# A long convolution as a two-stage 2048-point transform with relayout through DRAM, hardware gelu, resident weights and a list-scheduled order

## The chip, the cores and the metric

The kernel runs on one core of a Trainium2 chip. The metric is device time in microseconds (us); the profile's span is shorter by about 2 us. Engines: PE is TensorE (matmul), PEld its weight loads, DVE VectorE, ACT ScalarE, POOL GpSimd, SP the engine that issues most transfers. PSUM is the on-chip memory that the matmuls write (psall in the listings); SBUF holds the other tiles.

## The reference, cut to what matters

```python
x = A_q                                             # [1, 2048, 512] bf16
xn = _layernorm(x)
# A: causal 4-tap shift of k, times v, long convolution, gate by xn
k_shift = sum over t of k_pad[:, t:t+S, :] * shift_k[:, ks-1-t]
kv = k_shift * v
y = irfft(rfft(kv, 2S) * rfft(ssm_k, 2S))[:S] + kv * ssm_D      # per channel
s = xn * y
# B: gated feed-forward, Dm = 512, Df = 1792
h = gelu_tanh(xn @ w_gate) * (xn @ w_up)
g = silu(h @ w_down)
out = x + s * g
```

The feed-forward needs 448 + 224 matmuls of 128x128 weights by 512 columns. How many the convolution needs depends on the algorithm.

## The kernel before

The convolution is cut in four blocks of 512 rows. Each block is transformed by a dense 1024-point DFT matrix (built in the kernel), the blocks' spectra are multiplied pairwise on DVE, and each output block is one inverse transform:

```python
def fwd_passB_group(dlt, mr, bank):                 # filter spectra: 224 matmuls
    for i_, (kt, ht) in enumerate(kts):             # 4 or 8 per group
        trk.op("PE", lambda e, ...: e.matmul(PS[bank][:, :], lhsT=stat, rhs=HT_sb[:, ht, :], ...))
    trk.op("ACT", lambda e: e.activation(SPEC[:, HS(dlt), mr, :], PS[bank][:, :], ACTF.Identity, scale=wc), ...)
# ... fwd_passA_group: the same for kv, 128 matmuls

def build_products(c):                              # spectra, on DVE, 128x2048 bf16 each
    for k, (hs, ks) in enumerate(terms):            # c + 1 terms
        # ... four products into TMP, two to four sums into Yp

def inverse_mm_part(c, half):                       # 128 matmuls over all blocks
    # ... 8 matmuls per 128 output rows, rhs=Yp
```

GELU is built from ACT and DVE passes over 128x512 tiles, each `unit` being one of 56 (quarter of rows, block of Df):

```python
def g_A(u):   # PSUM (gate and up, 1024 columns) -> GUS                  ACT
def g_B1(u):  # SQ = (sqrt(a) g)^2                                       ACT
def g_T(u):   # SQ = SQ + 1                                              DVE
def g_B3(u):  # SQ = SQ * g                                              DVE
def g_C(u):   # SG = sigmoid(2c SQ)                                      ACT
def g_D(u):   # Wb = up * SG                                             DVE
def g_E(u):   # HTq = Wb * g                                             DVE
```

The program is emitted in a hand-made order: transforms first, then four quarters of the feed-forward with DVE's spectral products and the inverse transforms strewn between. Weights are loaded again for each quarter. A tracker puts in every semaphore wait from the tiles that an instruction reads and writes.

## Time and profile before

| | before |
|---|---|
| time, median (range) | 333.7 us (333.24 to 334.14) |
| span | 331.3 us |
| PE, DVE, ACT busy | 272.6, 266.2, 207.7 us |
| matmuls of 512 columns | 1160 |
| bytes moved | 34.8 MB |

From the page of the kernel before: busy time of each engine, three of the rows of 40 slices (a digit is the busy share of a slice of 8.3 us in tenths; PEclk is the granted TensorE clock in tenths), and the chain of waits that ended last.

```profile
PE 272.6 (82%) x1328; PEld 124.3 (38%) x1352; DVE 266.2 (80%) x473; ACT 207.7 (63%) x305; POOL 17.5 (5%) x33
...
PE   0235999999999969975878997968997998999970
...
DVE  6997899990069955999999899999999963766733
...
PEclk9999999999999979999999999999999999999995
...
PE 47%; DVE 35%; ACT 12%; issue 2%; DMA 2%; POOL 1%; POOLq 0%; ACTq 0%
```

PE is nearly full from the fifth slice on, with dents where DVE is full.

The groups of instructions by shape, kernel before: line, engine, operation, output<-inputs, shapes, count, then busy us and mean ns of one, then idle time before and what ended it.

```profile
L959 PE MATMUL psall<-XNTq,WBUF 128*128 128x512 bf16 x373 | 86.9, 383 | 11.1 <-ACT GUS L727 3.8 <-ACT XNTq L557 3.6 <-DMA WBUF<-in_B_w_gate_dram 2.7
L727 ACT ACTIVATE GUS<-psall 128x1024 bf16<-128x1024 f32 x56 | 56.8, 1014 | 22.7 <-PE psall L959 22.5
...
L436 DVE TENSOR_TENSOR TMP<-SPEC 128x2048 bf16<-128x2048 bf16 x40 | 47.5, 1215 | 19.3 <-ACT SPEC L604 19.3
...
L436 DVE TENSOR_TENSOR HTq<-Wb,GUS 128x512 bf16<-128x512 bf16 x56 | 23.8, 425 | 1.9
...
L436 DVE TENSOR_TENSOR G<-psall,SG 128x512 bf16<-128x512 f32 x16 | 9.9, 678 | 11.5 <-ACT SG L796 11.5
L436 DVE TENSOR_TENSOR XN_sb<-psall,XN_sb 128x1024 bf16<-128x1024 f32 x8 | 9.8, 1219 | 7.1 <-PE psall L812 7.1
```

A matmul's mean of 383 ns is the time from its start to its end in the profile, in which others run beside it. What it costs is the pitch, the time from one start to the next, which the windows show: busy time (and count) of PE, PEld, DVE, ACT, POOL, then clock, DMA share, GB/s.

```profile
40.00:60.00 20.00, 19.89 (x92) 9.09 (x93) 19.96 (x14) 8.24 (x12) 0.00 (x0) 1.00 0.00 0
...
160.00:200.00 40.00, 35.93 (x173) 16.00 (x176) 38.36 (x78) 25.50 (x38) 2.91 (x4) 1.00 0.41 129
```

92 matmuls in 19.9 us are 216 ns each. From 160 to 200 us both PE and DVE are almost full. So PE's 1160 matmuls alone are 250 us of the 331.

### The profile page before, as it was taken

The numbers are of one execution on the slowest core, as the hardware profiler recorded it, in microseconds if no ns is written. First come the engines' busy times: TensorE is split into PE (matmuls) and PEld (weight loads), VectorE is DVE, ScalarE is ACT, GpSimd is POOL, SyncE is SP. The second block draws the span as 40 slices with busy tenths as digits, with TensorE's granted clock in tenths as the row PEclk, the third lists the DMA queues.
The fourth block names the chain that finished last, engine by engine and source line by source line (L and its number), as shares of the span: only waits on it lengthen the run. The fifth ranks groups of instructions, "written<-read, shape, count | busy, mean of one in ns | idle before, by whom it ended". The sixth has DMA issues, their size and how long they took to land.

```text
span 331.3 us, 3631 instructions
## 1 busy us (share of the span) xinstructions
PE 272.6 (82%) x1328; PEld 124.3 (38%) x1352; DVE 266.2 (80%) x473; ACT 207.7 (63%) x305; POOL 17.5 (5%) x33
## 2 busy tenths in 40 slices
PE   0235999999999969975878997968997998999970
PEld 0005544444544424422333442424442344443420
DVE  6997899990069955999999899999999963766733
ACT  1498934443986745885629677637668928679820
POOL 2002300000000000000000200000020000120001
PEclk9999999999999979999999999999999999999995
DMA  7999200000000071534212745203643513653301
GB/s 243 264 252 256 65 1 0 2 0 0 2 0 0 2 253 31 161 127 128 96 34 94 232 161 177 74 23 127 190 120 136 160 63 127 190 141 116 95 0 63
DMA packets 52899, 34.83 MB, mean 105 GB/s; under 512 B 26257, under 2 KB 51858, under 8 KB 52882
## 3 DMA queue, kind: packets, MB, share of 16 engines
q1 hardware_dynamic: 51602, 30.42, 32.0%
q0 software_dynamic: 1280, 4.20, 3.9%
q8 instruction: 10, 0.16, 0.2%
q14 instruction: 7, 0.06, 0.0%
HBM read 26.22 MB, written 2.10 MB: 85 GB/s over the span
## 4 chain that ended last, share of the span: by engine, by line
PE 47%; DVE 35%; ACT 12%; issue 2%; DMA 2%; POOL 1%; POOLq 0%; ACTq 0%
PE psall L592 15%; PE psall L959 10%; DVE TMP L436 9%; PE psall L602 8%; PE psall L1034 8%; DVE Yp L436 7%; PE psall L812 4%; DVE HTq L436 4%; DVE Wb L436 3%; DVE SQ L436 3%; ACT GUS L727 3%; DVE G L436 2%; DVE SQ L737 2%; PE psall L531 2%; DVE XN_sb L436 2%
## 5 line engine op out<-in xcount | busy, mean ns | idle before, releaser
L959 PE MATMUL psall<-XNTq,WBUF 128*128 128x512 bf16 x373 | 86.9, 383 | 11.1 <-ACT GUS L727 3.8
L727 ACT ACTIVATE GUS<-psall 128x1024 bf16<-128x1024 f32 x56 | 56.8, 1014 | 22.7 <-PE psall L959 22.5
L436 DVE TENSOR_TENSOR TMP<-SPEC 128x2048 bf16<-128x2048 bf16 x40 | 47.5, 1215 | 19.3 <-ACT SPEC L604 19.3
L959 PEld LDWEIGHTS psall<-XNTq,WBUF 128*128 128x128 bf16 x384 | 36.6, 98 | 58.9 <-ACT GUS L727 9.4
L745 ACT ACTIVATE SG<-SQ 128x512 bf16<-128x512 bf16 x56 | 34.7, 621 | 26.9 <-DVE Wb L436 26.9
L592 PE MATMUL psall<-HT_sb,TT_sb 128*128 128x512 bf16 x219 | 48.1, 379 | 0.3
L1034 PE MATMUL psall<-WBUF,HTq 128*128 128x512 bf16 x188 | 43.4, 379 | 5.6 <-DVE HTq L436 5.2
L595 ACT ACTIVATE SPEC<-psall,COLS 128x512 bf16<-128x512 f32 x32 | 21.6, 700 | 25.3 <-PE psall L592 25.3
L733 ACT ACTIVATE SQ<-GUS 128x512 bf16<-128x512 bf16 x56 | 35.3, 630 | 1.8
L592 PEld LDWEIGHTS psall<-HT_sb,TT_sb 128*128 128x128 bf16 x224 | 21.9, 98 | 26.2
L1034 PEld LDWEIGHTS psall<-WBUF,HTq 128*128 128x128 bf16 x192 | 18.0, 98 | 30.4 <-DVE HTq L436 6.4
L812 PE MATMUL psall<-Yp,T_sb 128*128 128x512 bf16 x127 | 28.7, 379 | 0.1
L436 DVE TENSOR_TENSOR Yp<-Yp,TMP 128x2048 bf16<-128x2048 bf16 x24 | 28.5, 1215 | 0.0
L602 PE MATMUL psall<-KV_sb,TT_sb 128*128 128x512 bf16 x125 | 27.5, 379 | 0.4 <-ACT KV_sb L580 0.3
L567 DVE SCALAR_TENSOR_TENSOR acc<-kT_sb,SK,acc 128x2047 bf16<-128x2047 bf16 (+2 forms) x12 | 27.2, 2341 | 0.0
L737 DVE TENSOR_SCALAR SQ<-SQ 128x512 bf16<-128x512 bf16 x56 | 16.1, 288 | 12.2 <-ACT SQ L733 12.2
L436 DVE TENSOR_TENSOR HTq<-Wb,GUS 128x512 bf16<-128x512 bf16 x56 | 23.8, 425 | 1.9
L436 DVE TENSOR_TENSOR Wb<-GUS,SG 128x512 bf16<-128x512 bf16 x56 | 23.3, 415 | 0.2 <-ACT SG L745 0.2
L436 DVE TENSOR_TENSOR SQ<-SQ,GUS 128x512 bf16<-128x512 bf16 x56 | 23.2, 415 | 0.0
L604 ACT ACTIVATE SPEC<-psall 128x512 bf16<-128x512 f32 x32 | 18.7, 637 | 6.7 <-PE psall L602 6.7
L959 PE MATMUL psall<-XNTq,WDR 128*128 128x512 bf16 x64 | 15.2, 380 | 6.6 <-ACT GUS L727 6.6
L836 POOL DMA_DIRECT2D out_dram<-XR x8 | 5.9, 732 | 259.4 <-DVE XR L436 257.0
(65 smaller groups left out, 233.4 us busy)
## 6 DMA issues: line engine op xcount, KB each, us to landing
WBUF<-in_B_w_gate_dram SPq DMA_DIRECT2D x12, 512.0 KB, 3.8
WBUF<-in_B_w_up_dram SPq DMA_DIRECT2D x12, 512.0 KB, 4.8
WBUF<-in_B_w_down_dram SPq DMA_DIRECT2D x12, 512.0 KB, 3.8
X_sb<-in_A_q_dram SPq DMA_DIRECT2D x2, 1024.0 KB, 7.0
XR<-in_A_q_dram POOLq DMA_DIRECT2D x8, 256.0 KB, 3.3
out_dram<-XR POOLq DMA_DIRECT2D x8, 256.0 KB, 3.7
WDR<-in_B_w_gate_dram SPq DMA_DIRECT2D x4, 256.0 KB, 5.4
WDR<-in_B_w_up_dram SPq DMA_DIRECT2D x4, 256.0 KB, 2.8
```

Source lines behind the costliest of these rows:

```text
L436: trk.op(eng, lambda e: e.tensor_tensor(out_ap, a_ap, b_ap, op), r=r, w=w)
L567: trk.op("DVE", lambda e, kd=kd, sh=sh: e.scalar_tensor_tensor(out=acc[:, kd, sh:S_LEN], in0=kT_sb[:, kd, 0:S_LEN - sh], scalar=SK32[:, kd ...
L592: trk.op("PE", lambda e, kt=kt, ht=ht, stat=stat, i_=i_: e.matmul(PS[bank][:, :], lhsT=stat, rhs=HT_sb[:, ht, :], start=(i_ == 0), stop=(i ...
L595: trk.op("ACT", lambda e: e.activation(SPEC[:, HS(dlt), mr, :], PS[bank][:, :], ACTF.Identity, scale=wc), r=psr_all(bank) + [rCOLS], w=[rS ...
L602: trk.op("PE", lambda e, kt=kt, stat=stat: e.matmul(PS[bank][:, :], lhsT=stat, rhs=KV_sb[:, 4 * c + kt, :], start=(kt == 0), stop=(kt == 3 ...
L727: trk.op("ACT", lambda e: e.activation(GUS[:, sl, :], PS2(gb), ACTF.Copy), r=psr_2(gb), w=[rGUS[sl]])
L733: trk.op("ACT", lambda e: e.activation(SQ[:, sq, :], GSv(sl), ACTF.Square, scale=SQRT_A), r=[rGUS[sl]], w=[rSQ[sq]])
L737: trk.op("DVE", lambda e: e.tensor_scalar(SQ[:, sq, :], SQ[:, sq, :], 1.0, None, ALU.add), r=[rSQ[sq]], w=[rSQ[sq]])
L745: trk.op("ACT", lambda e: e.activation(SG[:, s2, :], SQ[:, sq, :], ACTF.Sigmoid, scale=GELU_2C), r=[rSQ[sq]], w=[rSG[s2]])
L812: trk.op("PE", lambda e, bank=bank, stat=stat, kr=kr: e.matmul(PS[bank][:, :], lhsT=stat, rhs=Yp[:, slot, kr, :], start=(kr == 0), stop=(k ...
L959: trk.op("PE", lambda e, bank=bank, stat=stat, kd=kd: e.matmul(PS[bank][:, :], lhsT=stat, rhs=XNTq[:, kd, :], start=(kd == 0), stop=(kd == ...
L1034: trk.op("PE", lambda e, bank=bank, mf=mf, jt=jt, buf=buf, mi=mi: e.matmul(PS[bank][:, :], lhsT=HTq[:, mf, 128 * jt:128 * (jt + 1)], rhs=b ...
```

## The change

Intent: fewer matmuls by a two-stage factorisation of the transform (16 x 128 points); relayout between the stages by writing scratch tensors to DRAM and reading them back in the other order; the product of the spectra taken straight from PSUM; gelu as one hardware function; weights loaded once; and an order found by a list scheduler in the program itself (tasks with estimated durations and priorities; it decides only the order of emission, the tracker still sets the waits). The core of the diff, cuts marked:

```diff
-        def g_A(u): ...   def g_B1(u): ...   def g_T(u): ...   def g_B3(u): ...
-        def g_C(u): ...   def g_D(u): ...    def g_E(u): ...
+        def unit(q, m):
+            # ... two halves of four matmuls each (gate, up) into one two-bank PSUM slot
+            op([("ACT", act(512))], lambda e, h: h.activation(GE[:, g.slot, :], ps(psl(p), 0), ACTF.Gelu_apprx_tanh), ...)
+            op([("DVE", dve(512, 1))], lambda e, h: h.tensor_tensor(HT[:, q % 2, m, :], ps(psl(p), 1), GE[:, g.slot, :], ALU.mult), ...)
-            # build_products, inverse_mm_part, fwd_passA_group, fwd_passB_group
+        def stage1(x, t, data, R_data, b_data, Z, prio):        # 16 times for the filter H, 16 for kv (K)
+            # ... 2 matmuls with F1[:, t, c, :] into a two-bank slot of pC
+            op([("ACT", act(1024)), ("DVE", dve(1024, 1))], ... copy(e, h, AST[:, a.slot, :, :]...))   # 3 staging buffers
+            S.add([("SP", 60.0)], st, r=[a], w=[bZ[x][t]], prio=prio, nbytes=262144)                    # store to ZH or ZK
+        for b in range(8):                                       # middle: load BH, BK from ZH, ZK
+            for pr in range(2):                                  # 16 steps
+                # K transform (2 matmuls, slot of pC) -> KB by ACT
+                # H transforms (2 + 2 matmuls, two slots) -> P1, P2 = PSUM * KB by DVE
+                # inverse (4 matmuls, a slot) -> BO by ACT or DVE -> store to ZI
+        # ... last stage: load BI from ZI, 32 matmuls, XN = PSUM * XN, output
+        pF = Pool_("psF", 2)                                     # PSUM slots of two banks each
+        pC = Pool_("psC", 2)
+        order = S.run()
+        for t in order:
+            t.emit(t.eng)
```

## The prediction

> **Now.** Span 331.3 us (page), 333.7 timed. PE busy 272.6 us, DVE 266.2, ACT 207.7 (busy table); the chain of waits is PE 47%, DVE 35%, ACT 12%. By windows: until 32 us DVE is full and PE nearly idle; from 40 to 100 us PE runs forward transforms at 216 ns a matmul (92 in 19.9 us); from 120 to 315 us PE is 84-98% busy, DVE full at 160-240.
>
> **The change, by program order.**
> PE: 512-column matmuls fall from 1160 to 928: gate/up 448 and down 224 stay, the convolution's 480 become 64 + 160 (middle) + 32 (last). At 216 ns that is 200 us, with 128 transposes about 210.
> DVE: spectral products (TMP, Yp: 86 us) and four GELU passes (SQ twice, Wb, HTq: 86 us) go. Added, at trace durations: 32 products PSUM x SBUF 128x1024 at 1.22 us (39 us); 56 HT multiplies at 0.68 us (38 us); 8 more PSUM passes (10 us). The shift is 32 passes of 1.215 us (39 us). Sum about 195.
> ACT: GELU becomes one 0.62 us pass instead of three (2.27 us); about 58 PSUM copies at 1.01 us. Sum about 120.
> DMA: weights load once, but three 4 MB scratch tensors are written and read: 40 MB, was 34.8. Each hop costs a landing of 2.6-3.8 us for 256-512 KB (DMA issue list); the Trainium skill, "DMA: Bandwidth & Descriptors" (anatomy of one DMA), gives about 2 us as fixed, and the trace agrees.
>
> **What lies on the critical path.** The order puts the engines partly in series:
> 1. Opening, DVE-bound. PE cannot start the first down projection before DVE has done tables, layernorm, 32 shift passes and 14 HT multiplies: tables and mask 15, layernorm 20, shift 39, evacuations 10, HT 9 = 93 us, plus about 11 of early waits for iotas and loads: 104 us (98-115). PE does only 144 of 928 matmuls here. The 14 MB of loads (50-55 us at the trace's 240-280 GB/s) and the stores queued behind should hide.
> 2. Then 696 matmuls x 216 ns = 150 us. The middle has four PSUM uses per step in two slots: an estimate of 4.2 us per step without interference, against 4.3-6 of PE work, so 12 us of stalls.
> 3. Tail: last scratch round trip mostly covered, then 88 matmuls (19 us) beside 21 us of DVE, last passes and landing: 29 us.
> Sum 295, plus 2.4 (timed minus span): **297 us, 281 to 318**, ratio 0.89.
>
> Chances: faster by over 2% 0.94, within 2% 0.03, slower 0.03.
>
> **What would show it.** DVE nearly full from 12 to 100 us, PE below half until 100, over 85% from about 105 to 265; the chain first DVE, then PE; HT 0.68 us, P products 1.22, GE 0.62; PE sum about 210, DVE 195; two ACT table loads, so gelu and tanh share one. Two-byte products from SBUF run at twice the rate of PSUM ones (Trainium skill, "VectorE: DVE Perf Modes", the perf-mode tier table; trace: 128x2048 SBUF 1215 ns, 128x1024 PSUM 1219); the shift's broadcast operand should keep that.
>
> **What would make it wrong.** Slower: broadcast or integer passes lose the fast rate (+17 to 25 us); stores queued behind the loads hold the three staging buffers and, through in-order ACT and PE, the first gate/up; two PSUM slots make the middle latency-bound at 6 us a step (+20). Faster: PE finds more to do in the opening, or no stalls in the middle: 280.

## The result, and the profile after

Ratios below are the mean time of one kernel's fast runs over that of the kernel before's fast runs of the same rounds, so not quite the ratio of the medians quoted. (The 333.7 us above was the median of three runs; here a fourth is added.)

| | before | after |
|---|---|---|
| time, median (range) | 333.85 us (333.24 to 334.14) | 279.62 us (278.94 to 280.19) |
| ratio | | 0.838 (0.836 to 0.841) |
| span | 331.3 us | 277.8 us |
| PE, DVE, ACT busy | 272.6, 266.2, 207.7 us | 218.3, 187.6, 118.1 us |
| matmuls of 512 columns | 1160 | 928 |
| bytes moved | 34.8 MB | 42.3 MB |

The direction was right; the time lies 1.4 us under the predicted range and 17 us under its centre. The page after (a slice is 6.9 us):

```profile
PE 218.3 (79%) x1056; PEld 100.9 (36%) x1056; DVE 187.6 (68%) x256; ACT 118.1 (43%) x141; POOL 17.4 (6%) x56
...
PE   0473003006999999999999999999999999999980
...
DVE  4999999897799953422332286767626477636996
...
PEclk9998555555999999999999999999999999999995
...
PE 74%; DVE 18%; ACT 2%; DMA 2%; POOL 1%; issue 1%; DVEq 0%
```

The reader sees two stretches with a sharp border in the tenth slice: before it DVE is full and PE idle, after it PE is at 9 without a dent. The prediction had PE "below half until 100".

Groups by shape, after:

```profile
L952 DVE TENSOR_TENSOR P<-psall,KB 128x1024 bf16<-128x1024 f32 x32 | 38.9, 1221 | 23.4 <-PE psall L519 22.9
L882 DVE TENSOR_TENSOR HT<-psall,GE 128x512 bf16<-128x512 f32 x56 | 38.3, 687 | 34.0 <-PE psall L519 33.8
L878 ACT ACTIVATE GE<-psall 128x512 bf16<-128x512 f32 x56 | 33.4, 597 | 41.7 <-PE psall L519 41.7
...
L847 DVE TENSOR_TENSOR KTM<-KK,SKB 128x2048 bf16<-128x2048 bf16 x12 | 14.6, 1218 | 0.2
```

Each unit cost was right within 4%: products 1.22 us, HT 0.69 us, gelu 0.60 us, and the shift's broadcast operand kept the fast rate (1218 ns for 2048 elements from SBUF, as the Trainium skill, "VectorE: DVE Perf Modes" (the perf-mode tier table), has it for two-byte products). So the error is in how the pieces lie beside each other. Windows after:

```profile
40.00:60.00 20.00, 2.74 (x18) 1.84 (x18) 18.61 (x29) 2.96 (x3) 2.16 (x2) 0.50 0.27 94
60.00:80.00 20.00, 15.29 (x58) 6.25 (x59) 16.22 (x31) 10.23 (x13) 2.55 (x4) 0.74 0.27 105
80.00:100.00 20.00, 20.00 (x130) 10.55 (x129) 19.17 (x22) 8.03 (x13) 0.00 (x0) 1.00 0.10 40
...
180.00:200.00 20.00, 20.00 (x95) 8.80 (x93) 13.73 (x15) 12.35 (x16) 0.00 (x0) 1.00 0.50 159
```

And PE's instructions in order of time around the border (start, duration, what, count, in brackets the idle time before and what ended it):

```profile
23.60 0.61 PE L519 MATMUL psall<-HTr,F 128*128 128x512 bf16 x2 [0.47 <-ACT AST L515]
45.23 1.89 PE L751 MATMUL psall<-ident,XN 128*128 128x128 bf16 x16 [21.03 <-ACT AST L515]
46.91 1.06 PE L519 MATMUL psall<-HTr,F 128*128 128x512 bf16 x2
64.71 1.03 PE L519 MATMUL psall<-HTr,F 128*128 128x512 bf16 x2 [16.74 <-DVE xnT L516]
65.54 1.91 PE L519 MATMUL psall<-xnT,Wg 128*128 128x512 bf16 x4
...
100.57 3.19 PE L519 MATMUL psall<-Wd,HT 128*128 128x512 bf16 x14
...
250.51 1.03 PE L519 MATMUL psall<-BI,G 128*128 128x512 bf16 x4
```

PE waits 16.7 us for one copy, xnT:

```profile
63.97 0.68 DVE L516 COPY xnT<-psall 128x1024 bf16<-128x1024 bf16 x1
```

DVE does it at 64.0 us because that is its place in DVE's in-order queue: behind 19 of the 32 passes of the shift stage and the layernorm of three quarters. From 64.7 us to the end of its work at 269 us PE hardly waits: it is busy for 203.5 of 204.3 us. (The chain of waits leaves PE there twice for 2.4 us, through two DVE passes each time, but PE has other work meanwhile: its own two waits are 0.8 us together.)

The prediction's sum against the trace:

| term | predicted | measured |
|---|---|---|
| opening, to the first down projection | 104 us | 100.6 us |
| from there to the last stage: 696 matmuls | 150 us | 149.9 us (100.57 to 250.51) |
| stalls of the middle stage | 12 us | 0, within the line above |
| tail | 29 us | 27.3 us |
| timed minus span of the profiled execution (280.17 - 277.8) | 2.4 us | 2.4 us |
| sum | 297 us | 280.2 us (median of all runs 279.6) |

Twelve of the seventeen missing microseconds are the stalls that did not come, and 1.7 us are in the tail. 3.4 us are in the opening. That its sum came so near looks like luck: the 100.6 us are 64.7 us until PE gets the xnT copy and 35.9 us in which PE is full, and not the list of DVE's work that the prediction added up. This mechanism needs checking, since it decides what could be gained there.

### The profile page after: what moved, and what is told of

Its sections match the earlier page's. It is cut to its first block, busy times and chain, and to the rows that moved or that the text cites. A ratio compares the mean times of both kernels' runs of the same rounds, so it can differ in the third digit from the quotient of the medians.

```text
span 277.8 us, 2849 instructions
## 1 busy us (share of the span) xinstructions
PE 218.3 (79%) x1056; PEld 100.9 (36%) x1056; DVE 187.6 (68%) x256; ACT 118.1 (43%) x141; POOL 17.4 (6%) x56
## 4 chain that ended last, share of the span: by engine, by line
PE 74%; DVE 18%; ACT 2%; DMA 2%; POOL 1%; issue 1%; DVEq 0%
PE psall L519 72%; DVE KAC L849 3%; DVE KTM L847 3%; DVE stats L726 2%; DVE F L585 2%; DMA X<-in_A_q_dram 2%; PE psall L779 1%; DVE G L906 1%; PE psall L751 1%; DVE V L851 1%; DVE F L584 1%; DVE KAC L843 1%; DVE XN L737 1%; POOL mv L733 1%; ACT AST L515 1%
## 5 line engine op out<-in xcount | busy, mean ns | idle before, releaser
L882 DVE TENSOR_TENSOR HT<-psall,GE 128x512 bf16<-128x512 f32 x56 | 38.3, 687 | 34.0 <-PE psall L519 33.8
L519 PE MATMUL psall<-xnT,Wg 128*128 128x512 bf16 x224 | 57.6, 384 | 0.8 <-DVE G L906 0.8
L519 PE MATMUL psall<-xnT,Wu 128*128 128x512 bf16 x224 | 57.6, 383 | 0.0
L952 DVE TENSOR_TENSOR P<-psall,KB 128x1024 bf16<-128x1024 f32 x32 | 38.9, 1221 | 23.4 <-PE psall L519 22.9
L878 ACT ACTIVATE GE<-psall 128x512 bf16<-128x512 f32 x56 | 33.4, 597 | 41.7 <-PE psall L519 41.7
L519 PE MATMUL psall<-Wd,HT 128*128 128x512 bf16 x224 | 50.8, 379 | 0.0
L515 ACT ACTIVATE AST<-psall 128x1024 bf16<-128x1024 f32 x26 | 26.2, 1022 | 39.9 <-PE psall L519 26.9
L519 PEld LDWEIGHTS psall<-xnT,Wg 128*128 128x128 bf16 x224 | 21.9, 99 | 27.9 <-DVE G L906 1.8
L519 PEld LDWEIGHTS psall<-xnT,Wu 128*128 128x128 bf16 x224 | 22.0, 99 | 26.6 <-issue 1.1
L519 PEld LDWEIGHTS psall<-Wd,HT 128*128 128x128 bf16 x224 | 21.9, 98 | 26.4 <-DVE G L906 0.2
L519 PE MATMUL psall<-HTr,F 128*128 128x512 bf16 x32 | 12.3, 494 | 18.6 <-DVE xnT L516 16.7
L849 DVE TENSOR_TENSOR KAC<-KAC,KTM 128x2048 bf16<-128x2048 bf16 x12 | 14.6, 1221 | 0.2
L847 DVE TENSOR_TENSOR KTM<-KK,SKB 128x2048 bf16<-128x2048 bf16 x12 | 14.6, 1218 | 0.2
```

The source lines that it names most:

```text
L515: return h.activation(o, i, ACTF.Copy)
L519: return h.matmul(o, lhsT=l, rhs=r, start=st, stop=sp)
L847: op([("DVE", dur)], lambda e, h, j=j, m=m: h.tensor_tensor(KTM[:, m.slot, :, :], kk(j), sk(j), ALU.mult), r=need + [bSKB, a], w=[m], rr=l ...
L849: op([("DVE", dur)], lambda e, h, m=m: h.tensor_tensor(KAC[:, a.slot, :, :], KAC[:, a.slot, :, :], KTM[:, m.slot, :, :], ALU.add), r=[m], ...
L878: op([("ACT", act(512))], lambda e, h: h.activation(GE[:, g.slot, :], ps(psl(p), 0), ACTF.Gelu_apprx_tanh), r=[p], w=[g], rr=lambda: [R_ps ...
L882: op([("DVE", dve(512, 1))], lambda e, h: h.tensor_tensor(HT[:, q % 2, m, :], ps(psl(p), 1), GE[:, g.slot, :], ALU.mult), r=[pu, p, g], w= ...
```

## The experiments

Theories at the outset. Theory 1: PE is short of work only until the xnT copy; from then on the matmul count sets the time, and the middle's two PSUM slots are covered by gate/up work beside them. Rivals: the sum of DVE's work bounds the opening to about 100 us (the prediction); stores queued behind loads hold it; the slots have so much slack that they never mattered. Three experiments compute a wrong result on purpose (m_nofill, p_kd3, s_tap1); the correctness check's tolerance let them pass, probably because x dominates the sum x + s*g, but they are no valid kernels.

### The opening: what does PE wait for?

**e_early**: put the first quarter's layernorm, transposes and their copies first in the list.

```diff
-  ... w=[bst[t]], rr=[R_X[t]], ww=[R_st[t]], prio=2)
+  ... w=[bst[t]], rr=[R_X[t]], ww=[R_st[t]], prio=-1 if q == 0 else 2)
   # the same at the five other tasks of this chain; the two small POOL memsets from prio=1 to 0
```

> Layernorm and transposes of the first quarter are put first in the list order (all else as in the change). Theory 1 (in the opening PE waits only for the place of one xnT copy in DVE's in-order queue, 64 us; afterwards PE is never short of work): first gate/up before 30 us, about 190 more matmuls (41 us) done before 65 us, time 240 to 252 us. Rival (the opening is bound by the sum of DVE's work to 99 us, as the prediction had it): PE only waits later, at the shift's results, and the time stays above 268 us.

Measured: 253.22 us (252.58 to 253.78), ratio 0.761 (0.758 to 0.763): 26 us faster than the changed kernel and 80 us faster than the one before, result correct. The first gate/up starts at 19.4 us. The first down projection and two windows of it:

```profile
54.93 9.23 PE L519 MATMUL psall<-Wd,HT 128*128 128x512 bf16 x41
...
30.00:65.00 35.00, 33.37 (x140) 14.70 (x144) 31.02 (x52) 11.70 (x18) 3.43 (x4) 0.90 0.49 156
65.00:90.00 25.00, 17.83 (x114) 8.42 (x114) 23.49 (x30) 16.42 (x19) 2.15 (x2) 1.00 0.36 137
```

PE now works through the stretch that was empty, and only 7 us are lost later, between 65 and 90 us. The time is 1.2 us above the expected range. The rival (above 268) is refuted: the first down projection starts at 54.9 us, when DVE has done 10 of the 32 shift passes (the last ends at 104 us). DVE's sum did not bound the opening, one place in its queue did. New priorities change the whole list order, so the next experiment keeps it.

**s_tap1**: compute only the first tap of the shift; order kept.

```diff
-  op([("DVE", dur)], ... KTM = kk(j) * sk(j) ...);  op([("DVE", dur)], ... KAC = KAC + KTM ...)
+  S.add([("DVE", dur)], lambda e: None, ...)       # both tasks stay in the schedule, emit nothing
```

> Only the first tap of the shift is computed (wrong result on purpose), 24 DVE passes fewer (29 us), of which 14 (17 us) stand ahead of the xnT copy that PE waits for. Theory 1: first gate/up at 47 to 50 us and time 14 to 17 us less (263 to 266). If the DVE sum of the whole opening mattered: 25 to 29 us less. If PE's start hangs on loads or stores instead: under 5 us less.

Measured: 261.49 us (261.07 to 261.81), ratio 0.786: 18.1 us less, one above the expected 14 to 17 and far from 25 to 29. PE's first gate/up of this run:

```profile
46.90 2.19 PE L519 MATMUL psall<-HTr,F 128*128 128x512 bf16 x4
48.89 1.65 PE L519 MATMUL psall<-xnT,Wg 128*128 128x512 bf16 x4
```

It starts 16.7 us earlier, and the time follows. The remaining 1.4 us fit a shorter stretch of half clock (below): after PE's restart the granted clock is 0.50 for 3.2 us here and for 5.8 us in the first profile of the changed kernel; half of the difference is 1.3 us. That was not tested by itself.

**e_zhq**: the 16 stores of the filter's scratch on another queue, so that they do not stand behind the loads.

```diff
-  dma(e, dst, AST[:, a.slot, :, :], d_ast[a.slot], ...)
+  dma("POOL" if x == "H" else e, dst, AST[:, a.slot, :, :], (d_asth if x == "H" else d_ast)[a.slot], ...)
```

> The 16 stores of the H scratch go out on POOL's queue and no longer stand behind the loads on SP's queue. Theory 1 (the xnT copy's place on DVE is what PE waits for): stores land well before 44 us, the 13 us wait of ACT for the store goes, but the first gate/up still starts at 64 to 65 us and the time is unchanged within 1 us. Rival (stores behind loads hold the staging buffers and so PE): first gate/up up to 13 us earlier and the time 8 to 13 us less.

Measured: 279.63 us (279.22 to 279.75), unchanged.

```profile
32.08 1.89 PE L751 MATMUL psall<-ident,XN 128*128 128x128 bf16 x16 [8.14 <-ACT AST L515]
33.76 1.06 PE L519 MATMUL psall<-HTr,F 128*128 128x512 bf16 x2
64.73 1.04 PE L519 MATMUL psall<-HTr,F 128*128 128x512 bf16 x2 [29.91 <-DVE xnT L516]
```

The stores did hold the transposes, by 13 us, as the prediction feared; taking that away only lengthens the wait for xnT from 16.7 to 29.9 us. A real wait, not on the critical path.

**e_iota, e_iota2, e_iota3**: why did one DVE pass of 0.43 us take 3.93 us? In the changed kernel DVE's passes over the table F show it:

```profile
6.52 3.93 DVE L585 TENSOR_SCALAR F<-F 128x1024 int16<-128x1024 int16 x1
...
11.07 0.70 DVE L585 TENSOR_SCALAR F<-F 128x1024 int16<-128x1024 int16 x1
...
12.40 0.43 DVE L585 TENSOR_SCALAR F<-F 128x1024 int16<-128x1024 int16 x1
```

POOL issues iotas back to back from 5.85 to 11.9 us. (The expectation below speaks of two passes stretched to 0.70 us; the trace has one.) e_iota:

```diff
-  S.add([("POOL", 16 * 250.0)], lambda e: iotas(1), w=[bIO[1]], prio=2)
+  S.add([("POOL", 16 * 250.0)], lambda e: iotas(1), r=bPH[0], w=[bIO[1]], prio=2)
```

> The second group of 16 iotas on POOL waits for the four first table passes of DVE. Theory (POOL beside DVE stretched one integer pass from 0.43 to 3.93 us and two to 0.70): those passes fall to 0.43 us, DVE's queue up to the xnT copy gets about 3.5 us shorter, time 3 to 4 us less (275.5 to 276.5). Rival (that pass is slow for another reason, or other waits fill the gap): pass still over 1 us, or time unchanged within 0.7 us.

Measured: 279.26 us, pass 4.20 us, nothing changed. e_iota2 did the same to the third group of iotas (`mt_pool`):

> A second try at what e_iota left untested: there other POOL work stood beside the slow DVE pass (4.20 us). Now all later iotas (both groups) wait until the four first table passes are done, so that POOL rests in that stretch. If POOL's stream of iotas stretches the pass: it falls from 3.9 to under 1 us, the first gate/up comes 3 us earlier and time is 2.5 to 3.5 us less. If the pass stays near 4 us, POOL's iotas are not its cause.

Measured: 279.35 us, pass 3.80 us. Both failed as experiments, and their traces say why: POOL still ran without a pause. A dependency of the list scheduler only orders emission; a semaphore wait arises only from a tile that both touch. e_iota3 adds such a resource:

```diff
+  R_phd = trk.free_res("phd")
   # the DVE pass over F:  w=rt  ->  w=rt + [R_phd];  the later iotas: r=[R_phd]
```

> e_iota and e_iota2 changed only the list order: their traces show that POOL did not wait, so the slow DVE pass beside it (3.8 to 4.2 us) stayed. Here the iotas wait for the table passes by a real semaphore. If POOL's instructions stretch that pass: it falls below 1 us, the first gate/up comes about 3 us earlier, time 2.5 to 4 us less than ctrl. If it stays near 4 us, POOL is not the cause.

Measured: 275.57 us (274.98 to 276.10), ratio 0.826, against 279.07 us (278.77 to 279.22), ratio 0.837, of the changed kernel: 3.5 us less.

```profile
6.53 0.43 DVE L585 TENSOR_SCALAR F<-F 128x1024 int16<-128x1024 int16 x1
```

The first gate/up starts at 61.4 us instead of 65.5. It is the wait that counts: e_iota2 gave the scheduler the same order without it and changed nothing. The Trainium skill, "SBUF — State Buffer" (SBUF: two separate sides), calls the port pair that DVE and GpSimd share "an exclusive lock, not a bandwidth split". The case agrees that POOL's work stops such a pass, and adds that a stream of short POOL instructions can hold it for over ten of them.

**w_warm, w_warm2 and ctrl**: 60 matmuls that nobody uses before the first gate/up.

```diff
+  if done[0] == 2:                       # after the first quarter's transposes
+      for k in range(60):
+          trk.op("PE", lambda h: mm(h, ps(0, k % 2), ident[:], Wg[:, 0, 0:512], True, True), ...)
```

> 60 matmuls on data that nobody uses fill PE's idle time before the first gate/up. If the low granted clock (0.5 in the slices from 28 to 62 us) carries over into the first useful matmuls (24 of them took 8.0 us from 64.7 us, 5.2 us at 216 ns), time 2 to 3 us less. If it only marks an idle PE: unchanged within 0.7 us.

Measured: 278.46 us (277.39 to 279.01), ratio 0.836 (0.833 to 0.839): not told apart from the changed kernel's 0.838 (0.836 to 0.841). Repeated with five rounds beside the changed kernel:

> w_warm again beside the changed kernel itself, since three rounds left it open (278.5 against 279.6 us). If half clock carries into the first useful matmuls: 2 to 3 us less than ctrl. If not: within 0.7 us of it.

> The changed kernel again, as the yardstick of this call: 279 to 280.3 us on any theory.

Measured: w_warm2 277.52 us (277.08 to 279.40), ratio 0.834 (0.831 to 0.836); ctrl 279.07 us, ratio 0.837 (0.835 to 0.838). The first useful matmuls of w_warm2:

```profile
64.23 0.61 PE L519 MATMUL psall<-HTr,F 128*128 128x512 bf16 x2 [2.87 <-DVE xnT L516]
64.68 1.03 PE L519 MATMUL psall<-xnT,Wg 128*128 128x512 bf16 x4
```

Four matmuls take 1.03 us there, 1.91 us in the changed kernel. So half clock did carry over, as the Trainium skill, "TensorE: Matmul & The Clock Gate" (Part 1), describes (half rate until about 3.4 us of sustained work). The mean gain is about 1.1 us, (0.8367 - 0.8335) x 333.7, below the 2 to 3 expected, and the intervals overlap. The traces show why it is hard to measure: how long the half clock lasts differs between executions of the same kernel. In the first profile of the changed kernel (280.17 us) the granted clock was 0.50 for 5.8 us from 64.7 us, in ctrl's (278.77 us) for 2.8 us from the same start:

```profile
67.26 1.16 PE L519 MATMUL psall<-HTr,F 128*128 128x512 bf16 x4
```

These four matmuls took 1.91 us in the first profile. So 14 matmuls ran at 427 ns there and 7 in ctrl, which at 211 ns extra each is an estimate of 2.9 and 1.5 us; the profiled execution of w_warm2 (277.08 us) is 3.1 and 1.7 us shorter than these two.

**early1_x1 and early1_x1_iota2**: also the second quarter first, and its part of x loaded earlier; then with the ordering of e_iota2.

```diff
-  prio=-1 if q == 0 else 2
+  prio=-1 if q <= 1 else 2               # all six tasks, as in e_early
+  load_x(1)                              # moved up, behind load_v(0)
```

> As e_early, and the second quarter's layernorm, transposes and load of x are put first too. In e_early PE stood from 69.8 to 82.8 us with 3.3 us of matmuls, waiting for staging copies and the second xnT. If PE's idle time in the opening is still the whole price: 6 to 10 us less than e_early's 253.2 us (243 to 247). If the shift's results (DVE to 103 us) and the slots of the middle now bind: within 2 us of 253.

> early1_x1 with the later iotas behind the first table passes. If DVE's two stretched passes at the start still lie ahead of PE's first gate/up: 2 to 4 us less than early1_x1. Else the same within 1 us.

Measured: 251.33 us (251.02 to 251.70), ratio 0.755, the fastest kernel and correct; and 255.94 us (254.54 to 256.38), ratio 0.769. early1_x1 missed the expected 243 to 247. From 65 to 90 us PE gained 4.5 us (22.3 busy, 17.8 in e_early), but from 90 to 130 us it lost 1.6, and after 200 us it stood 0.8 us longer. The second is slower although only an order changed and, as seen above, no wait was added. Its trace shows where: the later iotas delay the table G, ACT's four passes over it stand before the first gelu in ACT's in-order queue, and that gelu runs at 35.8 us instead of 30.8. PE waits 10.6 us for it, 3.4 in early1_x1, and restarts at 36.4 us instead of 31.5. These 5.0 us account for the 4.6 us between the times; this is read from the traces and not tested by a further run.

### The middle: where were the stalls?

**m_nofill**: the gate/up units of quarters 2 and 3 left out, to see the middle's own step.

```diff
-  for m in range(MF):
+  for m in range(MF if q < 2 else 0):
       unit(q, m)
   # and bHT[2:] = bHT[:2], so that the down projections read what is there
```

> Gate/up units of quarters 2 and 3 left out (wrong result on purpose; down projections of these quarters read the earlier quarters' tiles). The middle then runs with little or no other work on PE, so its own step is seen: the prediction's estimate was 4.2 us without interference, PE's own work is 10 matmuls (2.2 us). If the two PSUM slots limit it at 4.2 us: KB copies 4.1 to 4.5 us apart. In the changed kernel 18 to 22 matmuls a step (3.9 to 4.75 us) would then cover it, which explains that no stall was seen. Rival (the step alone is nearer 3 us, the slots never mattered): under 3.6 us apart.

Measured: 272.83 us (one run, state unknown). Its KB copies on ACT, a step apart:

```profile
198.00 1.02 ACT L515 ACTIVATE KB<-psall 128x1024 bf16<-128x1024 f32 x1 [1.33 <-PE psall L519]
...
202.08 1.02 ACT L515 ACTIVATE KB<-psall 128x1024 bf16<-128x1024 f32 x1 [1.33 <-PE psall L519]
```

In the changed kernel:

```profile
175.14 1.02 ACT L515 ACTIVATE KB<-psall 128x1024 bf16<-128x1024 f32 x1
...
179.82 1.02 ACT L515 ACTIVATE KB<-psall 128x1024 bf16<-128x1024 f32 x1 [1.13 <-PE psall L519]
...
184.63 1.02 ACT L515 ACTIVATE KB<-psall 128x1024 bf16<-128x1024 f32 x1
```

4.08 us a step alone, 4.75 us with filler. The prediction's 4.2 was near. But 4.75 us is also 22 matmuls of 216 ns: the ten of the step and three halves of a gate/up unit. The list order put just enough filler into each step to hide the slots. Leaving out 224 matmuls (48 us) saved only 7 us in total. PE's waits of this run tell what took their place: 11.0 us for DVE's products, 8.4 us for the BO copies that free a slot, 9.0 us for the last stage's loads from ZI. PE waits in a step both for a slot and for the products themselves, so how much of the 4.08 us is the slots and how much the chain of passes was not separated; no run had a third slot.

**m_kb2**: each KB copy done twice; order kept.

```diff
+  for _ in range(2):
       trk.op(e, lambda h: copy(e, h, KB[:, kb.slot, :, :]..., ps(psl(pk))), ...)
```

> Each KB copy done twice on ACT (order kept): the slot of the K transform is held 1.02 us longer in each of 16 steps. If the middle is balanced on the edge (slot cycle 4.2 us against 4.3 to 4.75 us of PE work): 8 to 14 us longer. If the slots have over 1 us of slack per step: within 2 us.

Measured: 288.94 us (288.82 to 289.07), ratio 0.869: 9.3 us longer. Steps go from 4.75 to 5.45 us on average (5.36 and 5.54 in turn):

```profile
182.16 2.08 ACT L515 ACTIVATE KB<-psall 128x1024 bf16<-128x1024 f32 x2 [1.13 <-PE psall L519]
...
187.70 2.07 ACT L515 ACTIVATE KB<-psall 128x1024 bf16<-128x1024 f32 x2
```

So 1.02 us more in the slots costs about 0.7 us a step: the slack was about 0.3 us. The middle stands at the edge.

**p_kd3**: gate/up contracts three of four blocks; order kept.

```diff
-  for kd in range(KD): ... kd == 0, kd == KD - 1
+  for kd in range(KD - 1): ... kd == 0, kd == KD - 2
```

> Gate/up contracts 3 of 4 blocks (wrong result on purpose): 112 matmuls fewer (24.2 us at 216 ns), order and all else kept. If PE alone binds from 65 us on: 22 to 25 us less (255 to 257). If the middle is at the edge of its slots, where over half of these matmuls lie, only 10 to 17 us less.

Measured: 265.00 us (263.82 to 265.63), ratio 0.798: 14.6 us less for 112 matmuls (24.2 us). The steps shrink to 4.41 us, although PE's share is 19 matmuls, 4.1 us. Fewer matmuls do not pay in full here: the slots and passes take over at 4.4 us. This agrees with m_kb2, since 4.41 + 1.02 is 5.43. Sixteen steps of 0.3 us are about 5 of the 9.6 us that are missing; at least 1.5 us more are in the opening (28 matmuls, 6.0 us, fewer, but the first down projection only 4.5 us earlier), and the rest was not followed.

### Does the time follow the matmuls?

**p_pad**: each gate/up half issues its first matmul three times; 224 matmuls more, result unchanged, order kept.

```diff
-  for kd in range(KD):
+  for n_, kd in enumerate((0, 0, 0, 1, 2, 3)):     # start=(kd == 0): the repeats overwrite
```

> Each gate/up half issues its first matmul three times (224 matmuls more, result unchanged, order kept): about as many matmuls as the change removed (232). If the time follows PE's matmul count from 65 us on: 48 us more (325 to 329 us), that is, about the kernel before. If PE has hidden slack in any stage: under 40 us more.

Measured: 325.98 us (325.82 to 326.32), ratio 0.977. Against 279.07 of the changed kernel, that is 46.9 us for 224 matmuls, 209 ns each, nearly the full pitch. Steps of the middle are then 6.04 us, 28 matmuls. With 1152 matmuls the new structure takes 326 us, where the old one takes 333.7 with 1160. At 209 ns each, the 232 matmuls that the change removed are an estimate of 48 of the 54 us gained. This is read from adding matmuls to the new kernel, where PE is full from 64.7 us on. The old kernel with fewer matmuls was not run, and there DVE was full beside PE for long stretches; so it is not shown that the count alone would have paid there, without the work that the change takes from DVE and ACT.

**b_gelu**: the kernel before with the hardware gelu alone.

```diff
-  e.activation(GUS[:, sl, :], PS2(gb), ACTF.Copy)
+  e.activation(GUS[:, sl, 0:DM], PS[gb][:, :], ACTF.Gelu_apprx_tanh)
-  tt("DVE", HTq[:, mf, :], Wb[:, s2, :], GSv(sl), ALU.mult, ...)
+  tt("DVE", HTq[:, mf, :], PS[ub][:, :], GSv(sl), ALU.mult, ...)
   # g_B1, g_T, g_B3, g_C, g_D gone; silu as (tanh(x/2) + 1) * x, halved in the filter's spectrum
```

> The kernel before with the hardware gelu alone (one ACT pass from PSUM, one DVE product; silu by tanh with the factor in the spectrum's scale). DVE loses 86 us of GELU passes and gains 38, ACT loses some 90 us; PE's 1160 matmuls stay (250 us). If the gain of the change comes from fewer matmuls (232 x 216 ns = 50 us of the 54): 310 to 325 us here (a few stretches where DVE was the limit). If the GELU is the main part: under 300 us.

Measured: fast runs 333.07 and 335.23 us (two more were slow), ratio 1.005 (0.997 to 1.012): the same. DVE's busy time fell from 266.2 to 227.2 us, ACT's from 207.7 to 120.7, and nothing was gained; the expected 310 to 325 was wrong. The waits of PE (total us, times, longest) and a piece of its timeline tell what PE waited for instead:

```profile
PE psall L960 <- DVE HTq L436: 12.4, 13, 2.8
```

```profile
147.36 1.90 PE L960 MATMUL psall<-XNTq,WBUF 128*128 128x512 bf16 x8 [0.97 <-DVE HTq L436]
```

PSUM is now freed by a DVE product that stands in queue behind 1.2 us spectral passes, where an ACT copy had freed it before. In the kernel before, PE waited 10.4 us in 12 times for that copy (GUS) and 5.2 us for HTq at the down projections. So one wait took the place of another of about the same size, and from 120 to 315 us PE was busy for 173.5 us, 174.3 before. With another order gelu alone might gain something in the old kernel; this run does not rule that out.

## Why the prediction was wrong

Right:
- Direction, and the main reason: fewer matmuls. In p_pad, 224 matmuls added to the new kernel bring back 46.9 of the 54 us.
- Unit costs: P products 1.22 us (predicted 1.22), HT 0.69 (0.68), gelu 0.60 (0.62). PE 218 us (predicted 210; part is half clock), DVE 188 (195), ACT 118 (120). Two ACT table loads.
- 696 matmuls at 216 ns: 149.9 us.
- The middle's own step: 4.2 us predicted, 4.08 measured (m_nofill). The offset of time and span: 2.4 us. Stores behind loads do hold the staging buffers.

Wrong, by the step as the prediction put it:
- "The middle has four PSUM uses per step in two slots: an estimate of 4.2 us per step without interference, against 4.3-6 of PE work, so 12 us of stalls." This term was 12 us and is 0. It is the main error. The two numbers beside each other already said that PE's work covers the slots, from 100.6 to 250.5 us PE stood for 0.8 us, and nothing says what the 12 us were read from. The prediction had named this way to be wrong itself ("no stalls in the middle: 280"). m_kb2 and p_kd3 show that the cover is thin: some 0.3 us a step.
- "Opening, DVE-bound ... 104 us". The step that failed is "PE cannot start the first down projection before DVE has done ... 32 shift passes": in e_early it starts after 10 of them, at 54.9 us, and 26 us go without taking any work from DVE. In the changed kernel PE waits for one copy at 64 us and then runs full. The sum was near (100.6 us) by luck; 3.5 us of a DVE pass held by POOL (e_iota3) and 1.5 to 2.9 us of half clock were in the measured time and not foreseen.
- The loads were put at 240 to 280 GB/s from the trace before; after, slices of the opening moved 345 to 400. DMA is 2% of the chain of waits, so this mattered little.
- The tail was 27.3 us for 29.

Left open: how the middle's 4.08 us divide between slots and the chain of passes, the rest of p_kd3's missing gain, and what fewer matmuls alone would have done in the old kernel.

## What to carry to other kernels

When one engine is followed by another through in-order queues, look for the single instruction whose place decides the start, and do not add up the first engine's whole load: moving a chain of small tasks forward was worth 26 us here, more than any unit cost in dispute. When a latency cycle (4.1 us of PSUM slots) runs beside filler work of another kind (4.75 us of matmuls), take the larger of the two and not a sum; beside the filler the cycle itself was 4.4 us here, so leave some room. And a dependency in a scheduler is not a wait on the chip: see in the trace that the experiment did what its edit meant.

## What the Trainium skill lacked or had wrong

- "SBUF — State Buffer" (SBUF: two separate sides) says that whichever op starts first holds the shared port pair for the whole instruction. It does not say what a stream of short POOL instructions does: a DVE pass of 0.43 us took 3.8 to 4.2 us beside back-to-back iotas of about 0.2 us, and 0.43 us again once they waited (e_iota3: 3.5 us of kernel time).
- "ScalarE: Activation LUTs" (Table sets) lists the gelu set as separate from gelu_apprx_tanh, but not which set holds the latter with tanh: here both ran to the end of the kernel after one load (1.28 us at 66.8 us; two loads in all, the first for sin).
- "TensorE: Matmul & The Clock Gate" (Part 1) agrees in kind. It puts the half rate at about 3.4 us of sustained work and says that this varies from run to run; here it lasted 5.8 us in one execution of the changed kernel and 2.8 us in another, 14 and 7 matmuls.
- No page says how a PSUM slot's cycle compares with filler work; measured: 4.08 us for four uses of two slots alone, 4.4 us at the least beside gate/up matmuls.
